# Windowed attention with its backward pass: x loads moved behind the token transpose, gradient loads held by GpSimd

## The chip, the cores and the metric

One core of one Trainium2 chip. The metric is the device time of one execution in microseconds.

## The reference

Windowed self-attention on an image of 256 x 256 tokens with 384 channels, windows of 8 x 8 tokens, one head, all in bfloat16, and its gradients:

```python
xw  = windows of x                       # 1024 windows, 64 tokens, C = 384
q, k, v = split(xw @ wqkv)
p   = softmax(q k^T * C**-0.5)
out = (p @ v) @ wo
# results: out, and the gradients of x, wqkv and wo for a given grad_out
```

## The kernel before

The kernel handles a "quad" of 8 windows (4 tiles of 128 tokens) at a time, 128 quads in all. Weights are multiplied together beforehand (A, B), so a quad needs x and grad_out in two layouts: tokens on the partitions (`xq`, `dq`) and channels on the partitions (`xT`, `dT`). The second layout comes from DMA transposes. The code below is cut and simplified, with my comments. Three quads are under way at once: in one step, quad a (= i+1) is projected, quad b (= i) has its softmax, quad c (= i-1) has its products with the probabilities and its stores.

```python
def load(st):
    st["xq"] = xq = grp.tile([P, QUAD, C], BF16, tag="xq", name="xq", bufs=2 * GQ + 4)
    st["dq"] = dq = qp.tile([P, QUAD, C], BF16, tag="dq", name="dq", bufs=6)
    for t in range(QUAD):
        nc.sync.dma_start(out=xq[:, t, :], in_=windows(x, st, 2 * t))              # SyncE's queue
        nc.gpsimd.dma_start(out=dq[:, t, :], in_=windows(grad_out, st, 2 * t))     # GpSimd's queue

def load_turn(st):      # two DMA transposes on SyncE's queue: dT<-dq, xT<-xq
def to_tokens(st):      # one DMA transpose on SyncE's queue: tok<-yz, 786 KB
def turn(st):           # one DMA transpose on SyncE's queue: PS<-ps, 131 KB

def step(c, b, a, ahead):
    # ... scores, softmax and uv of b; first projection of a (reads dT) ...
    B(turn)
    if ahead is not None:
        load(ahead)                 # quad i+3
    filler(1)
    C_(attend, (0, 1))              # six stores on GpSimd's queue
    # ... second projection of a (reads xT, ends yz) ...
    A(to_tokens)
    filler(1)
    C_(attend, (2, 3))              # six more stores on GpSimd's queue

for i in range(-1, n + 1):
    load_turn(sts[i + 2])           # first in the step
    step(get(i - 1), get(i), get(i + 1), get(i + 3))
    # ... collection of quads for the weight gradients left out ...
```

So SyncE's queue holds, in each step and in this order: dT, xT, PS, four x loads, tok. GpSimd's holds: four gradient loads, six stores, six stores. Both feed the same 16 DMA engines.

Of the kernel before, what the change touches and what calls it, by code (L numbers as in the profile page):

```python
# [11 lines left out]
BF16 = mybir.dt.bfloat16  # L12
F32 = mybir.dt.float32

P = 128
WIN = 8
WT = WIN * WIN
QUAD = 4
# [4 lines left out]
def kernel(  # L23
# [21 lines left out]
    nc = tc.nc  # L45
    _, H, W, C = x.shape
    CK = C // P
    J = 3 * C
# [4 lines left out]
    grp = ctx.enter_context(tc.tile_pool(name="grp", bufs=2 * GQ + 1))  # L53
# [53 lines left out]
    def windows(ap, st, first, count=2):  # L107
        row, col = st["at"]
        return ap[0, row + WIN * first:row + WIN * (first + count), col:col + WIN, :]
# [1 line left out]
    LO, HI = slice(0, WT), slice(WT, P)  # L111
    OTHER = {0: HI, WT: LO}

    def load(st):
        st["xq"] = xq = grp.tile([P, QUAD, C], BF16, tag="xq", name="xq", bufs=2 * GQ + 4)
        st["dq"] = dq = qp.tile([P, QUAD, C], BF16, tag="dq", name="dq", bufs=6)
        for t in range(QUAD):
            nc.sync.dma_start(out=xq[:, t, :], in_=windows(x, st, 2 * t))
            nc.gpsimd.dma_start(out=dq[:, t, :], in_=windows(grad_out, st, 2 * t))  # L119

    def load_turn(st):
        xq, dq = st["xq"], st["dq"]
        st["xT"] = xT = qp.tile([P, QUAD, CK, P], BF16, tag="xT", name="xT", bufs=3)
        st["dT"] = dT = qp.tile([P, QUAD, CK, P], BF16, tag="dT", name="dT")
        for src, dst in ((dq, dT), (xq, xT)):
            k = G_ON_PE if src is dq else 0
            if k < QUAD:
                nc.sync.dma_start_transpose(out=dst[:, k:].rearrange("p t m k -> p (t m) k"),
                                            in_=src[:, k:].rearrange("p t c -> p (t c)"))
# [34 lines left out]

    def to_tokens(st):
        st["tok"] = tok = qp.tile([P, CK, QUAD, 2, P], BF16, tag="tok", name="tok", bufs=3)
        nc.sync.dma_start_transpose(out=tok[:].rearrange("p m t b k -> p (m t b) k"),
                                    in_=st["yz"][:].rearrange("p m t s k -> p (m t s k)"))

    def scores(st):  # L170
        yz, xT = st["yz"], st["xT"]
# [7 lines left out]
    def over_k(ap, n=P):  # L179
        return ap.unsqueeze(2).broadcast_to([n, QUAD, WT])  # L180

    def soft(st, step):
        sd = st["sd"]
        if step == 0:
# [111 lines left out]
    def gf_group(sts):  # L296
        n = len(sts) * QUAD
        for f in range(2):
            for ma in range(CK):
                pw = ring.tile([P, C], F32, tag="r", name="pg")  # L300
                for i in range(n):
                    st, t = sts[i // QUAD], i % QUAD
                    product(pw[:], st["xq"][:, t, ma * P:(ma + 1) * P], st["UW"[f] + "q"][:, t, :], i == 0, i == n - 1)
                nc.vector.tensor_tensor(out=GF_acc[:, f, ma, :], in0=pw[:], in1=GF_acc[:, f, ma, :], op=ALU.add)  # L304
                yield

    def filler(n):
        while n and fill:
            try:
                next(fill[0])  # L310
                n -= 1
            except StopIteration:
                fill.pop(0)

    def step(c, b, a, ahead):


        def on(st):
            return (lambda f, *r: f(st, *r)) if st is not None else (lambda f, *r: None)
        C_, B, A = on(c), on(b), on(a)  # L320
        B(scores)
        B(soft, 0)
        B(uv, 0, 0)
        B(uv, 0, 1)
        B(soft, 1)
        B(uv, 1, 0)
        B(uv, 1, 1)
        B(soft, 2)
        B(soft, 3)
        B(uv, 2, 0)  # L330
        B(uv, 2, 1)
        for t in range(QUAD):
            A(grad_turn, t)
        B(uv, 3, 0)
        B(uv, 3, 1)
        B(soft, 4)
        for mo in range(CK):
            A(project, 0, mo)
        B(soft, 5)
        B(turn)  # L340
        if ahead is not None:
            load(ahead)
        filler(1)
        C_(attend, (0, 1))
        split[0] = True
        for mo in range(CK):
            A(project, 1, mo)
        A(to_tokens)
        filler(1)
        split[0] = ALL  # L350
        C_(attend, (2, 3))
# [3 lines left out]
    quads = [(row, col) for row in range(0, H, 2 * WIN * QUAD) for col in range(0, W, WIN)]  # L355
    sts = [{"at": q, "i": i} for i, q in enumerate(quads)]
    n = len(sts)
    AHEAD = 3
    with tc.manual_schedule(engines=MANUAL):
        for i in range(min(AHEAD, n)):  # L360
            load(sts[i])
            if i < AHEAD - 1:
                load_turn(sts[i])
        held = []
        get = lambda i: sts[i] if 0 <= i < n else None
        for i in range(-1, n + 1):
            if AHEAD - 1 <= i + AHEAD - 1 < n:
                load_turn(sts[i + AHEAD - 1])
            step(get(i - 1), get(i), get(i + 1), get(i + AHEAD) if i >= 0 else None)
            if i > 0:  # L370
                held.append(sts[i - 1])
                sts[i - 1] = None
            if held and (len(held) == GQ or i == n):
                fill.append(gf_group(held))
                held = []
        split[0] = False
        filler(1 << 30)
# [10 lines left out]
            nc.vector.tensor_copy(out=GFT[f][:, mb, :], in_=pt[:])  # L388
    dw_view = out_2.rearrange("(m p) j -> p m j", p=P)
    for ma in range(CK):  # L390
        dw_sb = grp.tile([P, J], BF16, tag="xq", name="dw_sb", bufs=2 * GQ + 4)
        for i, (lhs, rhs, r0) in enumerate(((GFT[0], w_sb, C), (GFb[0], w_sb, 0), (GFT[1], woT_sb, 0))):
            pe = ring.tile([P, C], F32, tag="r")
            for mb in range(CK):
                nc.tensor.matmul(pe[:], lhsT=lhs[:, mb, ma * P:(ma + 1) * P], rhs=rhs[:, mb, r0:r0 + C],
                                 start=(mb == 0), stop=(mb == CK - 1))
            if i < 2:
                nc.scalar.activation(out=dw_sb[:, i * C:(i + 1) * C], in_=pe[:], func=ACT.Copy, scale=scale)
            else:
                nc.vector.tensor_copy(out=dw_sb[:, i * C:(i + 1) * C], in_=pe[:])  # L400
        nc.sync.dma_start(out=dw_view[:, ma, :], in_=dw_sb[:])
# [38 lines left out]
```

## Time and profile before

| | before |
|---|---|
| time, median of the first runs | 1992.8 us (1986.3 to 1994.8) |
| span of the profiled run | 1989.7 us |
| undisturbed step (one quad) | 15.13 us |
| PE busy in such a step | 15.13 us |

The page gives shares over the whole span; the chain and the queue of SyncE give the step. PE is TensorE's matmuls, PEld its weight loads, DVE VectorE, ACT ScalarE, POOL GpSimd and SP SyncE. A row "SPq" of the timeline is an issue by SyncE: its duration is the time for which the issue holds SyncE, and not the time of the transfer (an x load holds it for some 0.6 us and lands 4.1 us after its issue began, in the median). "PE pu <- DMA PS<-ps" in a table of waits means that the matmul that writes pu stood idle until that transfer landed.

### The profile page before, as it was taken

Reading aid. Unit: us, or ns where it says so; the run is one execution under the profiler, and the core shown is the slowest. Engines: PE = TensorE matmul, PEld = TensorE weight load, DVE = VectorE, ACT = ScalarE, POOL = GpSimd, SP = SyncE. Lnnn points to the kernel's source line nnn. Section 1 sums busy time; section 2 is a strip of 40 time slices with the busy share of each in tenths; the row PEclk is TensorE's granted clock in tenths of the full one; section 3 lists DMA queues with packets and bytes.
Section 4 is the critical chain, followed back from the end, with each engine's and each line's share of the span. In section 5 each row is a group of like instructions: output and inputs, shape, how many; then the busy total and the mean of one; then the engine's idle time right before and its main releaser. Section 6 shows DMA issues by size and latency. Waiting matters only on the chain.

```text
span 1989.7 us, 52374 instructions
## 1 busy us (share of the span) xinstructions
PE 1961.3 (99%) x19418; PEld 1122.4 (56%) x19418; DVE 1258.1 (63%) x2851; ACT 1453.4 (73%) x3341; POOL 1122.6 (56%) x2054
## 2 busy tenths in 40 slices
PE   7899999999999999999999999999999999999998
PEld 4455555555555555555555555555555555555555
DVE  4666666666666666666666666566666666666665
ACT  5777777777777777777777777677777777777774
POOL 3555555565556555555655555555555556555543
PEclk9999999999999999999999999999999999999999
DMA  9999999999999999999999999999999999999993
GB/s 202 224 207 222 209 213 226 220 215 225 211 216 223 215 213 214 227 220 217 220 213 219 221 217 210 219 218 223 220 216 216 211 224 214 225 214 219 213 206 102
DMA packets 1042272, 425.62 MB, mean 214 GB/s; under 512 B 925792, under 2 KB 1016672, under 8 KB 1042016
## 3 DMA queue, kind: packets, MB, share of 16 engines
q1 hardware_dynamic: 943312, 270.60, 81.5%
q0 software_dynamic: 98304, 151.39, 31.3%
q8 instruction: 152, 2.49, 0.5%
q14 instruction: 104, 0.85, 0.1%
q10 hardware_dynamic: 400, 0.29, 0.0%
HBM read 101.84 MB, written 101.84 MB: 102 GB/s over the span
## 4 chain that ended last, share of the span: by engine, by line
PE 91%; DMA 7%; ACT 1%; DVE 1%; issue 0%; POOL 0%; SPq 0%; ACTq 0%; POOLq 0%
PE pj L147 33%; PE pj L145 12%; PE pg L147 12%; PE pg L145 12%; PE pd L258 6%; PE pu L253 5%; PE sd L147 5%; PE pw L253 4%; DMA dT<-dq 4%; DMA PS<-ps 2%; ACT uq L229 1%; ACT vq L229 0%; DMA dq<-in_grad_out_dram 0%; DMA xT<-xq 0%; PE pd L253 0%
## 5 line engine op out<-in xcount | busy, mean ns | idle before, releaser
L292 POOL DMA_DIRECT2D out_dram<-o x256 | 139.1, 543 | 693.8 <-ACT o L264 686.4
L304 DVE TENSOR_TENSOR GF_acc<-pg,GF_acc 128x384 f32<-128x384 f32 x258 | 143.8, 557 | 522.5 <-PE pg L145 372.3
L264 ACT CAST o<-po 128x384 bf16<-128x384 f32 x512 | 221.4, 487 | 248.1 <-issue 247.7
L147 PEld LDWEIGHTS <-xT 128*128 128x128 bf16 x3072 | 291.8, 98 | 182.2
L147 PE MATMUL pj<-B_sb,xT 128*128 128x384 bf16 x1536 | 333.4, 326 | 0.0
L147 PE MATMUL pj<-AT_sb,xT 128*128 128x384 bf16 x1536 | 333.3, 326 | 0.0
L119 POOL DMA_DIRECT2D dq<-in_grad_out_dram x512 | 274.2, 548 | 72.5 <-DMA out_dram<-o 39.1
L147 PE MATMUL pj<-dT,BT_sb 128*128 128x512 bf16 x1152 | 269.7, 379 | 5.5 <-DMA dT<-dq 5.3
L145 PE MATMUL pj<-xT,A_sb 128*64 128x512 bf16 x2304 | 271.9, 381 | 1.9 <-DMA xT<-xq 1.8
L229 ACT CAST uq<-pj 128x384 bf16<-128x384 f32 x512 | 247.3, 483 | 31.5 <-PE pj L147 28.4
L229 ACT CAST vq<-pj 128x384 bf16<-128x384 f32 x512 | 250.0, 488 | 2.7 <-ACT uq L229 0.3
L264 ACT CAST d<-pd 128x384 bf16<-128x384 f32 x512 | 227.6, 512 | 0.2 <-ACT o L264 0.2
L147 PEld LDWEIGHTS <-xq 128*128 128x128 bf16 x1572 | 153.7, 98 | 114.8 <-issue 0.3
L145 PEld LDWEIGHTS <-xq 128*64 128x64 bf16 x3000 | 167.9, 110 | 88.9
L207 ACT COPY ps<-Pb 64x256 bf16<-64x256 bf16 x256 | 103.2, 403 | 149.7 <-DVE Pb L204 148.2
L163 ACT CAST yz<-pj 128x512 bf16<-128x512 f32 x384 | 208.5, 659 | 3.6 <-PE pj L145 3.5
L161 ACT CAST yz<-pj 128x512 bf16<-128x512 f32 x384 | 206.4, 645 | 0.3 <-PE pj L147 0.2
L145 PEld LDWEIGHTS <-A_sb 128*64 128x64 bf16 x2304 | 132.4, 110 | 100.2 <-DMA xT<-xq 2.3
L147 PEld LDWEIGHTS <-BT_sb 128*128 128x128 bf16 x1152 | 111.4, 98 | 131.4 <-DMA dT<-dq 11.3
L147 PE MATMUL pg<-Uq,xq 128*128 128x384 bf16 x1032 | 181.6, 326 | 0.0
L253 PE MATMUL pu<-xq,PS 64*64 64x384 bf16 x1024 | 174.9, 335 | 6.4 <-DMA PS<-ps 5.9
L258 PE MATMUL pd<-tok,ps 128*64 128x384 bf16 x1024 | 177.7, 344 | 0.0
(68 smaller groups left out, 3366.6 us busy)
## 6 DMA issues: line engine op xcount, KB each, us to landing
xq<-in_x_dram SPq DMA_DIRECT2D x512, 96.0 KB, 4.1
dq<-in_grad_out_dram POOLq DMA_DIRECT2D x512, 96.0 KB, 4.0
out_dram<-o POOLq DMA_DIRECT2D x256, 96.0 KB, 4.3
out_dram<-o POOLq DMA_DIRECT2D x512, 48.0 KB, 4.4
out_dram<-d POOLq DMA_DIRECT2D x256, 96.0 KB, 4.4
out_dram<-d POOLq DMA_DIRECT2D x512, 48.0 KB, 4.4
dT<-dq SPq DMA_TRANSPOSE x128, 6.6
xT<-xq SPq DMA_TRANSPOSE x128, 6.8
```

The costliest lines, as they stand in the source:

```text
L119: nc.gpsimd.dma_start(out=dq[:, t, :], in_=windows(grad_out, st, 2 * t))
L145: nc.tensor.matmul(out[h], lhsT=lhsT[:, h], rhs=rhs, start=start, stop=stop)
L147: nc.tensor.matmul(out, lhsT=lhsT, rhs=rhs, start=start, stop=stop)
L161: ENG[EV["z"][mo]](out=yz[:, mo, :, 0:4:3, :], in_=pj[:])
L163: ENG[EV["y"][mo]](out=yz[:, mo, :, 1:3, :], in_=pj[:])
L207: nc.scalar.copy(out=ps[h, :, w, :], in_=Pb[h, :, :])
L229: cp(out=dst[:, t, :], in_=pj[:])
L253: nc.tensor.matmul(at[o, :], lhsT=turned(st, lhs, t, h), rhs=st[rhs][h, t, :], **{"start": True, "stop": True, **fl})
L258: nc.tensor.matmul(pd[outer if w == 0 else 1 - outer][o, :], lhsT=st["ps"][:, t, w, :], rhs=st["tok"][:, :, t, w, :], **flags)
L264: nc.scalar.copy(out=sb[:], in_=src[outer][:])
L292: nc.gpsimd.dma_start(out=windows(dst, st, 2 * t0 + 1), in_=sb[:])
L304: nc.vector.tensor_tensor(out=GF_acc[:, f, ma, :], in0=pw[:], in1=GF_acc[:, f, ma, :], op=ALU.add)
```

## The change

The intent is to keep loads away from the large token transpose: the x loads stand behind it in SyncE's queue, and GpSimd is held, by a copy of one element that reads the transpose's first part, until two thirds of it have landed.

```diff
-    def load(st):
-        st["xq"] = xq = grp.tile(..., bufs=2 * GQ + 4)
+    def load(st, behind=None):
+        st["xq"] = xq = grp.tile(..., bufs=2 * GQ + 5)
         st["dq"] = dq = qp.tile(..., bufs=6)
+        if behind is not None:
+            nc.gpsimd.tensor_copy(out=dq[0:1, 0, 0:1], in_=behind[0:1, 0, 0, 0, 0:1])
     ...
     def to_tokens(st):
         st["tok"] = tok = qp.tile([P, CK, QUAD, 2, P], ...)
-        nc.sync.dma_start_transpose(out=tok[:]..., in_=st["yz"][:]...)
+        for m in (slice(0, CK - 1), slice(CK - 1, CK)):
+            nc.sync.dma_start_transpose(out=tok[:, m]..., in_=st["yz"][:, m]...)
     ...
         B(turn)
-        if ahead is not None:
-            load(ahead)
         filler(1)
         C_(attend, (0, 1))
     ...
         A(to_tokens)
+        if ahead is not None:
+            load(ahead, a["tok"])
         filler(1)
     ...
-            step(get(i - 1), get(i), get(i + 1), get(i + AHEAD) if i >= 0 else None)    # AHEAD = 3
+            step(get(i - 1), get(i), get(i + 1), get(i + 4))
```

(The dots and the comment on AHEAD are mine. The loads ahead of the loop are rewritten to the same effect; cut.)

More of the change, by code (lines that the diff above doesn't have):

```diff
@@ L112 @@
     OTHER = {0: HI, WT: LO}
-    def load(st):
-        st["xq"] = xq = grp.tile([P, QUAD, C], BF16, tag="xq", name="xq", bufs=2 * GQ + 4)
+    def load(st, behind=None):
+        st["xq"] = xq = grp.tile([P, QUAD, C], BF16, tag="xq", name="xq", bufs=2 * GQ + 5)
         st["dq"] = dq = qp.tile([P, QUAD, C], BF16, tag="dq", name="dq", bufs=6)
+        if behind is not None:
+            nc.gpsimd.tensor_copy(out=dq[0:1, 0, 0:1], in_=behind[0:1, 0, 0, 0, 0:1])
         for t in range(QUAD):
@@ L166, in to_tokens @@
         st["tok"] = tok = qp.tile([P, CK, QUAD, 2, P], BF16, tag="tok", name="tok", bufs=3)
-        nc.sync.dma_start_transpose(out=tok[:].rearrange("p m t b k -> p (m t b) k"),
-                                    in_=st["yz"][:].rearrange("p m t s k -> p (m t s k)"))
+        for m in (slice(0, CK - 1), slice(CK - 1, CK)):
+            nc.sync.dma_start_transpose(out=tok[:, m].rearrange("p m t b k -> p (m t b) k"),
+                                        in_=st["yz"][:, m].rearrange("p m t s k -> p (m t s k)"))
     def scores(st):
@@ L357 @@
     n = len(sts)
-    AHEAD = 3
     with tc.manual_schedule(engines=MANUAL):
-        for i in range(min(AHEAD, n)):
-            load(sts[i])
-            if i < AHEAD - 1:
-                load_turn(sts[i])
+        load(sts[0])
+        load_turn(sts[0])
+        load(sts[1])
+        load_turn(sts[1])
+        load(sts[2])
         held = []
@@ L366 @@
         for i in range(-1, n + 1):
-            if AHEAD - 1 <= i + AHEAD - 1 < n:
-                load_turn(sts[i + AHEAD - 1])
-            step(get(i - 1), get(i), get(i + 1), get(i + AHEAD) if i >= 0 else None)
+            if 0 <= i < n - 2:
+                load_turn(sts[i + 2])
+            step(get(i - 1), get(i), get(i + 1), get(i + 4))
             if i > 0:
@@ L390 @@
     for ma in range(CK):
-        dw_sb = grp.tile([P, J], BF16, tag="xq", name="dw_sb", bufs=2 * GQ + 4)
+        dw_sb = grp.tile([P, J], BF16, tag="xq", name="dw_sb", bufs=2 * GQ + 5)
         for i, (lhs, rhs, r0) in enumerate(((GFT[0], w_sb, C), (GFb[0], w_sb, 0), (GFT[1], woT_sb, 0))):
```

## The prediction

> **What bounds the kernel now.** I read the page first, then the chain in order of time, two windows of one step each, the waits of PE and the issue queue of SyncE.
>
> The busy row and two of the slice rows of the page:
>
> ```profile
> PE 1961.3 (99%) x19418; PEld 1122.4 (56%) x19418; DVE 1258.1 (63%) x2851; ACT 1453.4 (73%) x3341; POOL 1122.6 (56%) x2054
> ...
> PEclk9999999999999999999999999999999999999999
> DMA  9999999999999999999999999999999999999993
> ```
>
> Two things are full at once: PE (99% of the span, at full clock) and the 16 DMA engines. The chain, in order of time, gives the step:
>
> ```profile
> 168.36 5.84 PE pj L147 x33
> 183.49 5.84 PE pj L147 x33
> 198.62 5.89 PE pj L147 x33
> ```
>
> The same 33 matmuls return every 15.13 us: one quad of windows. The two windows below are one such step each (columns: stretch, length, busy time of PE, PEld, DVE, ACT, POOL, clock, DMA share, GB/s):
>
> ```profile
> 1019.66:1034.79 15.13, 15.13 (x153) 8.70 (x152) 9.70 (x23) 11.29 (x27) 8.78 (x16) 1.00 1.10 218
> 1034.79:1049.92 15.13, 15.13 (x153) 8.69 (x152) 9.70 (x23) 11.29 (x27) 8.79 (x16) 1.00 1.18 193
> ```
>
> PE has no idle time in an undisturbed step, so 15.13 us is a floor that no ordering of transfers can lower. 128 quads x 15.13 = 1936.6 us; the rest of the 1989.7 us span is start, end and disturbed steps. I took the start of the first score matmul of every quad from the trace: from quad 3 on, 20 of 124 steps are longer than 15.15 us, together by 11.9 us. That sum is all that a better order of transfers can win in the steady part: 0.6% of the time. The waits name who made it:
>
> ```profile
> PEld L147 <- DMA dT<-dq: 11.3, 17, 1.5
> PEld L253 <- DMA PS<-ps: 9.0, 12, 3.5
> PE pu L253 <- DMA PS<-ps: 5.9, 5, 3.2
> PE pj L147 <- DMA dT<-dq: 5.3, 9, 1.1
> ```
>
> The gradient transpose (dT) and the probability transpose (PS) come late now and then. (Weight-load and matmul rows show the same late transfer twice and are not to be added.) Why they are late is in SyncE's issue queue:
>
> ```profile
> 1055.64 5.33 SPq L167 DMA_TRANSPOSE tok<-yz  x1
> 1061.19 2.63 SPq L128 DMA_TRANSPOSE dT<-dq  x1
> 1064.00 3.79 SPq L128 DMA_TRANSPOSE xT<-xq  x1
> 1067.95 1.19 SPq L233 DMA_TRANSPOSE PS<-ps  x1
> 1069.20 2.51 SPq L118 DMA_DIRECT2D xq<-in_x_dram  x4
> 1071.82 4.83 SPq L167 DMA_TRANSPOSE tok<-yz  x1
> ```
>
> There is no gap: SyncE issues all the time, about 10.5 us behind the point where the program could have it. The token transpose of a quad is issued at 20.3 us after the start of the step that made its input at 12.8 us. So the queue is not waiting for data; it drains as fast as the DMA engines take it. Over the trace the mean issue times in one step are dT 2.22, xT 3.02, PS 1.50, x 2.73 and tok 4.86 us, 14.3 us, and with about 0.8 us between them the step is full. dT lands at about 17.5 us after its step began and must be there at 19.7 (4.6 us into the next): some 2 us to spare, and the stalls are the steps where that is used up.
>
> **What the Trainium skill says.** "DMA: Bandwidth & Descriptors", section "Queues, rings and completion order", says that each DMA engine round-robins between its queue rows packet by packet. So loads from GpSimd's queue take turns with the transposes of SyncE's. The trace agrees: the token transpose takes between 5.8 and 12.3 us to land (median 8.4) for always the same 786 KB, depending on what runs beside it. "Perfetto Trace Analysis", section "What 'DMA-bound' means", counts as DMA-bound a kernel whose issuing sequencer is a solid row of DMA slices; SyncE's row is that here, beside a full PE. "GPSIMD Engine Reference", section "3.1 Elementwise — side-by-side cycle accounting", gives about 156 ns of dispatch per instruction; no GpSimd copy of one element stands in the trace of before.
>
> **The change part by part.**
> 1. The four x loads (0.6 us of issue each) move from before the token transpose to behind it and are for quad i+4 instead of i+3. Same number and bytes. The token transpose goes 2.7 us earlier in SyncE's cycle, the next dT comes at the same place of the cycle. Cost 0. The buffer count goes from 10 to 11 with the distance, so the buffer waited for is released by the same group of weight-gradient products as before. No new wait.
> 2. The token transpose becomes two. One more issue on a full SyncE. The smallest PS issue, 131 KB, takes 1.19 us, the smallest dT issue, 393 KB, 1.42 us: about 1.1 us is fixed (1.19 less half of the 0.23 that 262 KB more cost). If none were hidden the step would be 16.2 us and the kernel 128 x 1.1 = 140 us slower. But a transpose lands 4 to 5 us after its issue ends, so work is queued in the engines while the next issue is prepared, and the 1.1 us falls into time that SyncE otherwise spends pushed back (tok takes 4.07 us at least, the others 1.2 to 1.5). I take 0.1 us as exposed.
> 3. GpSimd copies one element from the first part of tok into dq: an estimate of 0.2 us from the page's dispatch, on an engine that is busy 8.8 of 15.13 us. Cost 0 on the path.
> 4. The wait. The first part, issued at about 17.6 us of its step, should land near 24.5, 9.4 us into the next step. Then GpSimd issues four gradient loads (4 x 0.55 = 2.2 us), then six delayed stores (3.3 us) and the six of the next half (3.3 us): 9 us of work before the next gate 15.13 us later, so it keeps up. The loads, issued 3.7 us into a step now, go out some 6 us later in relation to the products, but are for one quad further. They land within 7 us, near 31 to 34 us after their step began; their dT is issued at 10.5 us two steps later, at 40.8. Spare 7 us. The stores (2,3) go out 11 us late; their eight buffers last two steps, 30 us. Spare over 10 us.
> 5. The gain. Sorting 120 steps by how far behind SyncE is, its next cycle takes on average 15.52 us where dT is issued before 10.3 us, 15.39 at 10.3 to 10.7, and 15.02 to 15.06 at 11.2 to 12.4. Early, the token transpose runs into the gradient loads; later, it misses them. The gate makes it miss them always. So I expect a natural SyncE cycle near 14.9 us (an estimate: 15.04 less something for the overlap that is still in there, plus the 0.1), below the 15.13 of PE. Then the queue catches up, dT lands well ahead, and the 11.9 us of stalls mostly go.
>
> Sum: 1992.8 less about 9 of the 11.9 us = 1984 us.
>
> **The rivals.**
> *A: the queue gets slower than PE.* The margin of the cycle is about 0.1 to 0.2 us. If the second issue costs more than 0.3 us, or if the now bunched traffic of GpSimd (loads, late stores, next stores in one run of 9 us from the landing of the first part on) slows dT and xT by more than tok gains, the cycle is over 15.13 and every step waits for dT. 15.3 us would be 2005 us or more (0.17 x 128 = 22 us on top of 1984), 15.5 us about 2030. For it: dT follows the x loads directly and so falls into the bunch. Against it: bytes and their kinds are unchanged, and the engines never were empty.
> *B: nothing moves.* The late steps come in bursts (steps 14 to 18, 79 to 82, 100 to 103, 120 to 124), each beginning with a step in which everything lands 2 to 5 us late at once. If something outside the order of these transfers causes them, they stay, and the time is 1990 to 1994.
> *C: the gate starves the gradient.* dq arrives too late for dT and the wait for dT becomes one for dq. It needs the 7 us of spare to go; then each step would lose, and I would see over 2050. Unlikely.
> *D: over 2% faster.* That is below 1953 us, and without any stall the kernel needs 1992.8 - 11.9 = 1981, perhaps 1978 if the first steps fill better. It would need PE to be shorter, and no matmul is changed.
>
> **Range and chances.** The low end is the floor with a little for the spread of runs (before: 1986.3 to 1994.8): 1977. The high end allows rival A with a cycle of about 15.3 us: 2010. Faster by over 2%: 0.01. Slower by over 2% (over 2032.7, a cycle of 15.5): 0.05. Within: 0.94.
>
> **What would show each step.** PE still 15.13 us in an undisturbed step; if that moved, the reading of the bound is wrong. Right on the gain: PE waits for dT and PS below 5 us, SyncE showing gaps or real waits before tok or PS, dT issued earlier than 10.5 us, tok landing (first issue to last landing) below 8 us. Step 2 wrong: the two tok issues together above 5.5 us while SyncE stays solid. Step 4 wrong: dT or PE waiting for the gradient load, or ACT waiting for an output buffer. Rival A: over half of the steps longer than 15.2 us with dT as releaser. What would make the prediction wrong altogether is a DMA cycle that leaves 15.13 us upward, since PE has nothing left to give.

## The result, and the profile after

The changed kernel takes 2101.5 us (2091.3 to 2104.4, 4 runs) against 1993.8 us of the kernel before in the same rounds: ratio 1.0537, with a 95% interval of 1.0494 to 1.0579. It is slower by 5.4%. (A ratio here is the mean time of one kernel's fast runs over the mean of the other's fast runs of the same rounds, so it is not quite the ratio of the medians quoted beside it.)

The busy row of the page after, and the waits of PE:

```profile
PE 1979.7 (95%) x19418; PEld 1117.3 (53%) x19418; DVE 1258.0 (60%) x2851; ACT 1457.3 (70%) x3341; POOL 1140.0 (55%) x2179
```

```profile
PE pu L256 <- DMA PS<-ps: 40.5, 40, 2.0
PE pj L149 <- DMA dT<-dq: 39.7, 47, 3.0
```

PE has the same 19418 matmuls and is now idle for 5% of the span. It waits for the same two transposes as before (5.9 and 5.3 us then). From quad 3 on, 92 of 124 steps are longer than 15.2 us (17 before), and all that exceeds 15.13 us adds up to 110 us (11.9 before). The other steps still take 15.13 us. So the floor has not moved; the queue in front of it has become slower than it. SyncE's queue, one cycle of the kernel after, from token transpose to token transpose:

```profile
1060.42 5.32 SPq L170 DMA_TRANSPOSE tok<-yz  x2
1065.79 2.57 SPq L120 DMA_DIRECT2D xq<-in_x_dram  x4
1068.60 1.45 SPq L130 DMA_TRANSPOSE dT<-dq  x1
1070.10 3.13 SPq L130 DMA_TRANSPOSE xT<-xq  x1
1073.39 2.28 SPq L236 DMA_TRANSPOSE PS<-ps  x1
1075.76 5.12 SPq L170 DMA_TRANSPOSE tok<-yz  x2
```

The row is still solid. In the mean over the steps of quads 20 to 110, from the start of one issue to the next:

| us per step | dT | xT | PS | tok | x loads | cycle |
|---|---|---|---|---|---|---|
| before | 2.33 | 3.20 | 1.54 | 5.15 | 2.97 | 15.18 |
| after | 1.96 | 3.68 | 1.92 | 5.34 | 3.15 | 16.05 |

The landing times say the same (transposes of the table of issues, before and then after; last column: median us from issue to landing):

```profile
xT<-xq SPq DMA_TRANSPOSE x128, 6.8
tok<-yz SPq DMA_TRANSPOSE x128, 8.4
PS<-ps SPq DMA_TRANSPOSE x128, 5.0
```

```profile
tok<-yz SPq DMA_TRANSPOSE x256, 5.4
...
xT<-xq SPq DMA_TRANSPOSE x128, 8.2
PS<-ps SPq DMA_TRANSPOSE x128, 5.6
```

(5.4 is for each of tok's parts; from the first part's issue to the last landing it is 7.9 us.) The token transpose gained half a microsecond, xT lost 1.4 and PS 0.6. PS has a deadline too: it landed 21.3 us after the start of its step before and 25.2 after (medians of the trace), and an undisturbed step reads it at 24.0.

And GpSimd's queue after, at the gate that waits for the token transpose issued at 1060.42 above:

```profile
1067.32 0.18 POOL L118 COPY dq<-tok 1x1 bf16<-1x1 bf16 x1 [2.24 <-PE pj L147]
1067.89 2.14 POOL L121 DMA_DIRECT2D dq<-in_grad_out_dram  x4 [0.39 <-POOL dq L118]
1069.98 0.57 POOL L295 DMA_DIRECT2D out_dram<-o  x1
```

The four x issues run from 1065.79 to 1068.36. GpSimd issues its loads only from 1067.89 on, then the held stores: their data move when SyncE is at dT, xT and PS. What does that leave beside the x loads? Four windows of 3 us before and four after, each beginning about 1 us after the first issue of a row of x loads (last two columns: mean busy share of the 16 DMA engines, GB/s):

```profile
977.47:980.47 3.00, 3.00 (x18) 1.59 (x17) 2.23 (x6) 1.78 (x6) 2.92 (x6) 1.00 0.98 234
992.50:995.50 3.00, 3.00 (x18) 1.57 (x16) 2.13 (x6) 1.78 (x5) 2.73 (x6) 1.00 0.97 268
1007.98:1010.98 3.00, 3.00 (x18) 1.57 (x16) 2.45 (x7) 1.81 (x5) 2.37 (x5) 1.00 0.89 229
1022.98:1025.98 3.00, 3.00 (x17) 1.56 (x16) 2.32 (x7) 1.78 (x6) 2.52 (x5) 1.00 1.10 204
```

```profile
1018.52:1021.52 3.00, 3.00 (x44) 1.83 (x41) 0.43 (x1) 1.39 (x3) 1.74 (x4) 1.00 1.16 148
1034.86:1037.86 3.00, 3.00 (x36) 1.80 (x32) 0.04 (x1) 1.87 (x5) 0.33 (x2) 1.00 1.15 140
1051.24:1054.24 3.00, 3.00 (x43) 1.68 (x40) 1.21 (x3) 1.01 (x4) 1.67 (x4) 1.00 0.87 159
1066.79:1069.79 3.00, 3.00 (x36) 1.79 (x32) 0.04 (x1) 1.87 (x5) 2.08 (x5) 1.00 0.88 189
```

204 to 268 GB/s before, 140 to 189 after. (The share counts a packet where it starts and is noisy over 3 us; the bytes are plain.) POOL is busy issuing for 2.4 to 2.9 of the 3 us before and 0.3 to 2.1 after: most of the missing bytes are GpSimd's. I laid the packets of 90 such rows over one another and took how busy the engines were in each microsecond, counted from the first x issue; in brackets, the part of GpSimd's queue. Over 1.00 means that packets overlap in an engine, and a stretch of transposes alone reaches 1.25.

| microsecond after the first x issue | 1 to 2 | 2 to 3 | 3 to 4 | 4 to 5 |
|---|---|---|---|---|
| before | 1.12 (0.57) | 1.04 (0.59) | 0.99 (0.52) | 0.99 (0.43) |
| after | 1.05 (0.04) | 0.82 (0.05) | 0.74 (0.18) | 0.86 (0.39) |

In the changed kernel the DMA engines run partly dry behind every row of x loads.

### The profile page after: what moved, and what is told of

Its sections match the earlier page's. It is cut to its first block, busy times and chain, and to the rows that moved or that the text cites. A ratio compares the mean times of both kernels' runs of the same rounds, so it can differ in the third digit from the quotient of the medians.

```text
span 2089.5 us, 52866 instructions
## 1 busy us (share of the span) xinstructions
PE 1979.7 (95%) x19418; PEld 1117.3 (53%) x19418; DVE 1258.0 (60%) x2851; ACT 1457.3 (70%) x3341; POOL 1140.0 (55%) x2179
## 5 line engine op out<-in xcount | busy, mean ns | idle before, releaser
L149 PE MATMUL pj<-dT,BT_sb 128*128 128x512 bf16 x1152 | 270.3, 380 | 54.2 <-DMA dT<-dq 39.7
L118 POOL COPY dq<-tok 1x1 bf16<-1x1 bf16 x125 | 22.1, 177 | 538.4 <-PE pj L147 302.2
L147 PE MATMUL pj<-xT,A_sb 128*64 128x512 bf16 x2304 | 278.0, 387 | 0.1
L256 PE MATMUL pu<-xq,PS 64*64 64x384 bf16 x1024 | 174.7, 335 | 41.1 <-DMA PS<-ps 40.5
L149 PEld LDWEIGHTS <-BT_sb 128*128 128x128 bf16 x1152 | 106.3, 98 | 195.1 <-DMA dT<-dq 82.5
L292 POOL DMA_DIRECT2D out_dram<-o x256 | 148.6, 581 | 90.0 <-DMA dq<-in_grad_out_dram 31.9
L295 POOL DMA_DIRECT2D out_dram<-o x256 | 141.3, 552 | 92.8 <-DMA dq<-in_grad_out_dram 52.7
```

The source lines that it names most:

```text
L147: nc.tensor.matmul(out[h], lhsT=lhsT[:, h], rhs=rhs, start=start, stop=stop)
L149: nc.tensor.matmul(out, lhsT=lhsT, rhs=rhs, start=start, stop=stop)
L256: nc.tensor.matmul(at[o, :], lhsT=turned(st, lhs, t, h), rhs=st[rhs][h, t, :], **{"start": True, "stop": True, **fl})
L292: nc.gpsimd.dma_start(out=windows(dst, st, 2 * t1 + 1, 1), in_=sb[LO, :])
L295: nc.gpsimd.dma_start(out=windows(dst, st, 2 * t0 + 1), in_=sb[:])
```

## The experiments

All 16 kernels are correct. The first theories were: **issue** (the second issue of the token transpose costs time on a full SyncE), **gate** (holding GpSimd bunches its traffic), **order** (the new place of the loads costs). Four kernels take the parts away one by one. (The diffs are cut to the lines that matter; the splitting of `load` into `load_x` and `load_d` is left out.)

**split_only**: the kernel before, with only the split.

```diff
-        nc.sync.dma_start_transpose(out=tok[:]..., in_=st["yz"][:]...)
+        for m in (slice(0, CK - 1), slice(CK - 1, CK)):
+            nc.sync.dma_start_transpose(out=tok[:, m]..., in_=st["yz"][:, m]...)
```

> The kernel before with the token transpose in two issues (2/3 and 1/3) and nothing else changed. Theory 'issue': the second issue costs the full SyncE queue some 0.8 us a step, so 2070 to 2100 us, and the two issues of tok together take over 5.6 us. Theories 'gate' and 'order': the extra issue hides in the backpressure, 1985 to 2000 us.

Measured: 2029.1 us (before 1995.1), ratio 1.0151, 95% interval 1.0102 to 1.0200. Between the two: the split costs something, less than the issue theory asked. The two issues of tok do not take longer than the one did (5.00 us against 5.15, from start to next start). The dT behind them takes 0.63 us longer (2.96 against 2.33) and PS 0.29, while xT takes 0.42 less: 0.3 us a step in all. PE then waits for PS above all (30.5 us in the trace, against 7.2 for dT).

**no_gate**: the changed kernel without the copy.

```diff
-            load(ahead, a["tok"])
+            load(ahead)
```

> The changed kernel without GpSimd's copy: the gradient loads stand at their new place in GpSimd's program (behind the first half's stores) but wait for no transpose; the split and the new place of the x loads stay. Theory 'gate': the loss is gone, 1985 to 2000 us. Theories 'issue' and 'order': still 2080 to 2105 us.

Measured: 2094.0 us, ratio 1.0495 (1.0452 to 1.0537). The gate is not the cause of the loss. Taking it away wins nothing that this run can tell from noise.

**whole_gate**: the changed kernel with one token transpose, all of which GpSimd waits for.

```diff
-        for m in (slice(0, CK - 1), slice(CK - 1, CK)):
-            nc.sync.dma_start_transpose(out=tok[:, m]..., in_=st["yz"][:, m]...)
+        nc.sync.dma_start_transpose(out=tok[:]..., in_=st["yz"][:]...)
```

> The changed kernel with the token transpose in one issue again; GpSimd then waits for all of it. Theory 'issue': 1985 to 2010 us. Theory 'gate': as slow or slower than the changed kernel, 2095 to 2130 us, since the gate opens about 1.5 us later. Theory 'order': 2085 to 2105 us.

Measured: 2031.0 us, ratio 1.0172 (1.0134 to 1.0209). All three theories missed: a gate that opens later is much better, though not good.

**order_only**: both of these edits; only the place of the loads is new.

> No split and no gate: only the loads moved behind the token transpose, four quads ahead. Theories 'issue' and 'gate': 1980 to 2000 us. Theory 'order' (x loads directly ahead of dT and xT, gradient loads behind the stores): 2085 to 2105 us.

Measured: 2074.9 us, ratio 1.0395 (1.0354 to 1.0436). PE waits 52.5 us for PS and 23.3 for dT. Most of the loss, 80 of 106 us, is in the part that I had called free: the order. With 2075 as the base, the whole gate wins 44 us and the split costs 19; both together lose 27.

So the order had to be taken apart. The second round's theory was **slot**: four x issues take 2.7 us whatever runs beside them, so GpSimd's traffic is free there and costs time beside transposes.

**x_only**: only the x loads go behind the token transpose; the gradient loads keep their place.

```diff
         B(turn)
-        if ahead is not None: load(ahead)            # x and gradient, i+3
+        if near is not None: load_d(near)            # gradient, i+3
     ...
         A(to_tokens)
+        if ahead is not None: load_x(ahead)          # x, i+4
```

> No split, no gate: only the x loads go behind the token transpose, four quads ahead; the gradient loads keep their old place in GpSimd's program, three ahead. Theory 'slot' (the issue of the x loads takes 2.7 us whatever runs beside it, so GpSimd's traffic that falls there is free, and what falls beside the transposes lengthens them): the gradient loads at 4 to 6 us of the step now fall beside tok and not beside x, so 2030 to 2080 us, with under 1.0 us of GpSimd's queue beside the x issues (1.6 before). Theory 'late loads' (what costs is that the gradient loads are issued at the end of the step, behind the stores): 1985 to 2005 us.

Measured: 2026.0 us, ratio 1.0149 (1.0123 to 1.0175), just below the slot theory's range; 0.94 us of GpSimd's queue beside the x issues, as it expected. Here the engines do not run dry behind the row: laid over one another as above, they are 1.19, 1.10, 1.04 and 1.03 busy in its second to fifth microsecond. This half of the order costs some 28 us in another way (see the sums below).

**dq_only**: the other half, x loads at the old place, gradient loads behind the first half's stores.

```diff
         B(turn)
-        if ahead is not None: load(ahead)
+        if near is not None: load_x(near)            # x, i+3
     ...
         A(to_tokens)
+        if ahead is not None: load_d(ahead)          # gradient, i+4
```

> No split, no gate: only the gradient loads go to their new place in GpSimd's program, four quads ahead; the x loads stay ahead of the token transpose, three ahead. Theory 'slot': the gradient loads leave the x loads and fall beside dT and xT at the end of the step, so 2030 to 2080 us and under 1.0 us of GpSimd's queue beside the x issues. Theory 'x order' (what costs is that the x loads stand directly ahead of dT): 1985 to 2005 us.

Measured: 1987.0 us, ratio 0.9949 (0.9919 to 0.9979): not slower but slightly faster. The expectation failed in its arithmetic, not in its rule: when the gradient loads go later, the stores behind them do too, and 1.70 us of GpSimd's queue still lies beside the x issues (1.61 in the kernel before). Neither half of the order costs 80 us. Together they do, because only together do they leave the row of x loads alone: in order_only 0.47 us of GpSimd's queue lies beside it.

**gate_PS**: the new order, no split, and the gate opens earlier, when PS has landed.

```diff
-            load(ahead, a["tok"])        # GpSimd waits for the token transpose of quad a
+            load_x(ahead)
+            load_d(ahead, b["PS"][0:1, 0, 0, 0:1])       # GpSimd waits for PS of quad b
```

> The changed order in one token transpose, with GpSimd's copy waiting for the probability transpose of the step instead of the token transpose: the gate opens some 3 to 4 us earlier, when the x loads are about to be issued, so that gradient loads and x loads move side by side. Theory 'slot': GpSimd's queue beside the x issues rises above 1.2 us, and the time goes below the kernel with the gate on the whole transpose (2031 us): 1990 to 2025 us. Theory 'bunch' (any holding of GpSimd costs): 2031 us or more.

Measured: 2004.8 us, ratio 1.0039 (1.0005 to 1.0074); 1.11 us of GpSimd's queue beside the x issues. In the slot theory's range of time, a little under its share. Holding GpSimd costs little (0.4%) if it is let go when the x loads start. Among the kernels with a row and no split, GpSimd's share beside the row and the time go together roughly: 0.47 us and 2075 (order_only), 0.94 and 2026 (x_only), 1.1 and 2031 (whole_gate), 1.11 and 2005, 1.61 and 1995 (before), 1.70 and 1987 (dq_only). In whole_gate that share must be stores, for its gradient loads may start only after tok has landed, 9.6 us after its issue, and by then the row has been issued.

**split_three**: the kernel before with the token transpose in three issues.

```diff
-        for m in (slice(0, CK - 1), slice(CK - 1, CK)):      # as in split_only
+        for m in (slice(0, 1), slice(1, 2), slice(2, 3)):
```

> The kernel before with the token transpose in three issues. If an extra transpose issue has a cost of its own (34 us for the first one, measured), a second extra issue doubles it: 2055 to 2075 us. If the 34 us came from the change of phase alone, the third issue adds little: 2020 to 2040 us.

Measured: 2035.6 us, ratio 1.0195 (1.0169 to 1.0221). That is 38 us over its kernel before, against 34 for two issues: the third adds nothing clear of noise. The split's cost is not a price per issue.

The third round tests the cause behind the slot. The theory **underfed**: an x issue takes 0.6 us for 98 KB, so SyncE supplies 393 KB in 2.7 us, 146 GB/s, while the kernel as a whole moves 217 GB/s; in a row of four the work queued in the engines runs out.

**x_eight**: the kernel before with the x loads in eight issues of 49 KB.

```diff
-            nc.sync.dma_start(out=xq[:, t, :], in_=windows(x, st, 2 * t))
+            for h, half in enumerate((LO, HI)):
+                nc.sync.dma_start(out=xq[half, t, :], in_=windows(x, st, 2 * t + h, 1))
```

> The kernel before with the x loads in eight issues of one window each, 49 KB, in place of four. Theory 'underfed': the row of x issues grows from 2.7 to some 5 us and feeds the engines at half the rate, GpSimd's traffic covers only a part: 2060 to 2200 us. Theory 'mixing': the same bytes at the same place, 1990 to 2020 us.

Measured: 2362.2 us, ratio 1.1837 (1.1793 to 1.1880), above the range that the theory gave. A cycle of its queue:

```profile
1003.94 5.13 SPq L119 DMA_DIRECT2D xq<-in_x_dram  x8
1009.17 5.55 SPq L168 DMA_TRANSPOSE tok<-yz  x1
```

Half the bytes take the same 0.6 us of SyncE: eight issues take 5.13 us where four took 2.5. The engines are still 1.14 and 1.08 busy in the second and third microsecond of the row and fall to 0.73, 0.47 and 0.33 in the fourth to sixth. The row is 2.5 us longer than before, the step 3.1. The same bytes, in the same place of the queue, cost 18% because they are issued in smaller pieces. The rival "mixing", that asked for 1990 to 2020 us, is out as the only cause.

**spread**: the kernel before with one x load behind each of the four transposes. (A sketch of the queue, not the code; the same in after_spread.)

```diff
-   SyncE's queue:  dT  xT  PS  x0 x1 x2 x3  tok
+   SyncE's queue:  dT  x0  xT  x1  PS  x2  tok  x3
```

> The kernel before with its four x loads spread over SyncE's queue, one behind each of the four transposes, instead of four in a row; the gradient loads stay. Theory 'underfed' (four x issues in a row, 0.6 us each for 98 KB, feed the 16 DMA engines too slowly; only traffic of GpSimd at that moment keeps them full): each single issue is covered by the transpose ahead of it, SyncE's cycle falls below 15.0 us, the stalls of PE go: 1977 to 1990 us. Theory 'mixing' (loads beside transposes slow these, so x loads and gradient loads must meet): 2010 us or more.

Measured: 2038.3 us, ratio 1.0207 (1.0178 to 1.0237), five rounds. The theory underfed missed this one wholly. The engines are well fed here, and yet SyncE's cycle is 15.5 us. What grew is the work: see the table of sums below.

**after_spread**: the same spread in the changed kernel, split and gate left as they are.

```diff
-   SyncE's queue:  dT  xT  PS  tok(2/3)  tok(1/3)  x0 x1 x2 x3
+   SyncE's queue:  dT  x1  xT  x2  PS  x3  tok(2/3)  tok(1/3)  x0
```

> The changed kernel (split, gate on the first two thirds, four ahead) with its x loads spread, one behind each transpose. Theory 'underfed': the low stretch of the DMA engines behind the x issues (0.74 to 0.86 busy) is gone, and with it most of the loss: 1985 to 2040 us, where the upper end is the cost of the split alone. Theory 'bunch' (held and late traffic of GpSimd beside dT and xT is the cost): 2080 us or more.

Measured: 1979.1 us (1978.5 to 1981.3), ratio 0.9915 (0.9892 to 0.9938), five rounds: faster than both kernels, below the expected range. Its queue, one cycle:

```profile
1010.93 5.90 SPq L174 DMA_TRANSPOSE tok<-yz  x2
1016.88 0.93 SPq L118 DMA_DIRECT2D xq<-in_x_dram  x1
1018.04 2.48 SPq L132 DMA_TRANSPOSE dT<-dq  x1
1020.57 0.58 SPq L118 DMA_DIRECT2D xq<-in_x_dram  x1
1021.25 1.55 SPq L132 DMA_TRANSPOSE xT<-xq  x1
1022.85 0.98 SPq L118 DMA_DIRECT2D xq<-in_x_dram  x1
1023.93 1.29 SPq L240 DMA_TRANSPOSE PS<-ps  x1
```

dT and xT together are issued in 4.0 us, 4.6 in the cycle shown of the kernel after. The queue catches up: dT is issued 10.2 us after the start of the step in step 6, 3.2 us in step 16, and stays near there (medians: 3.6 here, 11.1 in the kernel before, where the prediction says about 10.5, and 14.1 in the one after). That is 0.70 us gained per step, a cycle of some 14.4 us as long as nothing holds it. Then the token transpose waits for its own input (its issue begins at 12.3 us of the step, as the second third of yz is written; it was 21.5 in the changed kernel), and PE, over its steps, only for itself: 2 of 124 steps are longer than 15.15 us.

That left open which part of the change the spread made useful. Three more kernels complete the table.

**spread_no_gate**: after_spread without GpSimd's copy.

```diff
-            load_d(ahead, a["tok"])
+            load_d(ahead)
```

> The changed kernel with its x loads spread, and GpSimd's copy left out (the split stays). Theory 'both' (a row of x issues starves the DMA engines, and gradient loads beside the token transpose lengthen it; the gate cures only the second and shows its worth once the first is cured): slower than the spread kernel with the gate (1979 us) by 10 to 60 us. Theory 'feed alone': the same within 6 us.

Measured: 2070.3 us, ratio 1.0366 (1.0304 to 1.0427). Slower, as the theory 'both' said, but by 91 us and not by 10 to 60.

**spread_whole_gate**: after_spread with the token transpose in one issue (the edit of whole_gate).

> The changed kernel with its x loads spread and the token transpose in one issue, so that GpSimd waits for all of it. If the split has a cost of its own wherever it stands (34 us in the kernel before), SyncE's slack must hide it in the spread kernel and nothing is to be seen: 1977 to 1984 us, with the token transpose issued no later. If the opening after two thirds is what makes the gate work, 1990 us or more.

Measured: 1977.0 us (1976.7 to 1977.9), ratio 0.9904 (0.9857 to 0.9951). The fastest by its median, though it and after_spread were not timed in the same rounds. Within the first range; opening after two thirds is not what makes the gate work.

**spread_order**: both edits.

> The changed kernel with its x loads spread, no split, no gate: the loads' places alone. Theory 'both': 1990 to 2040 us. Theory 'feed alone': 1977 to 1985 us.

Measured: 2037.5 us, ratio 1.0213 (1.0144 to 1.0282), at the upper end of the range of 'both'. It loads four quads ahead and spread three, and both take the same time (2037 and 2038 us), so the distance is not likely to matter; no run changed it alone.

**split_reverse**: a last look at the split: the kernel before, one third of the token transpose first, two thirds last.

```diff
-        for m in (slice(0, CK - 1), slice(CK - 1, CK)):      # as in split_only
+        for m in (slice(0, 1), slice(1, CK)):
```

> The kernel before with the token transpose in two issues, one third first and two thirds last. With two thirds first the gradient transpose behind it took 0.6 us longer to issue, in two parts as in three (where the last part is one third as well). If a short last part is what costs, this one is near the kernel before: 1990 to 2010 us. If any cut of the token transpose costs: 2022 to 2040 us.

Measured: 1997.2 us (before 1998.5), ratio 0.9998 (0.9975 to 1.0022). And **split_dT**, run with the third round, with the gradient transpose in two issues:

```diff
-            nc.sync.dma_start_transpose(out=dst[:]..., in_=src[:]...)
+            for g in (slice(0, 2), slice(2, 4)) if src is dq else (slice(0, 4),):
+                nc.sync.dma_start_transpose(out=dst[:, g]..., in_=src[:, g]...)
```

> The kernel before with the gradient transpose, not the token transpose, in two issues. If any additional transpose issue costs what the split of tok cost, 2025 to 2040 us; if that cost belongs to tok's place and phase, 1990 to 2010 us.

Measured: 1996.2 us, ratio 1.0000 (0.9968 to 1.0031). So one more transpose issue costs nothing by itself in these two places. A short piece at the end of the token transpose, directly ahead of dT, costs 34 us.

### The table that they make

Medians in us, loads at their new place in all eight; the kernel before was at 1994 to 1998 in these rounds:

| | x loads in a row | x loads spread |
|---|---|---|
| no split, no gate | 2075 | 2037 |
| split, no gate | 2094 | 2070 |
| no split, gate on all of tok | 2031 | 1977 |
| split, gate on the first two thirds | 2101 (the change) | 1979 |

The gate is worth 44 us with the row and no split, 60 with the spread and no split, 91 with spread and split, and nothing in the one combination that the change chose.

Two sums from the traces sort the kernels. A packet is one piece of a transfer in the trace (256 bytes in a transpose). Add up the time of all DMA packets of a step and divide by 16 engines: that is the work. Divide the work by the step: that is how full the engines are. This is bookkeeping: it tells which of the two moved, not why. Packets overlap in an engine, so a packet's time can hold waiting for others; and where PE sets the step (15.13 us), fullness says only how much work there was.

| | step, us | packet time, us | fullness |
|---|---|---|---|
| before | 15.18 | 17.55 | 1.156 |
| after | 16.03 | 17.79 | 1.110 |
| no_gate | 16.06 | 17.78 | 1.107 |
| split_only | 15.49 | 17.90 | 1.155 |
| x_only | 15.50 | 18.36 | 1.184 |
| dq_only | 15.22 | 17.93 | 1.178 |
| order_only | 15.85 | 17.62 | 1.112 |
| whole_gate | 15.52 | 17.37 | 1.119 |
| gate_PS | 15.23 | 16.93 | 1.112 |
| x_eight | 18.24 | 18.39 | 1.008 |
| spread | 15.53 | 18.29 | 1.177 |
| spread_order | 15.55 | 18.09 | 1.163 |
| spread_no_gate | 15.75 | 18.19 | 1.155 |
| spread_whole_gate | 15.13 | 17.32 | 1.145 |
| after_spread | 15.13 | 17.33 | 1.145 |

A row of x loads with nothing beside it goes with a low fullness (after, no_gate, order_only), and so does a row of eight issues (x_eight). That is not the whole cause: x_only and split_only are as full as the kernel before or fuller and lose some 30 us because the work grew, and gate_PS is as little full as order_only and loses almost nothing because its work is the least of all. Spreading the x loads restores the fullness, but without a gate the work goes up: a 256-byte packet of a transpose takes 27.3 ns on average in spread and 25.5 in spread_whole_gate, and with 6656 such packets on 16 engines in a step, 1.8 ns are 0.75 us.

A gate takes work back in three of the four pairs (17.62 to 17.37, 18.09 to 17.32, 18.19 to 17.33; 17.78 to 17.79 in the fourth), and not by a faster token transpose. From order_only to whole_gate (each time first without, then with the gate):

```profile
dT<-dq SPq DMA_TRANSPOSE x128, 6.6
...
tok<-yz SPq DMA_TRANSPOSE x128, 7.6
```

```profile
dT<-dq SPq DMA_TRANSPOSE x128, 5.2
...
tok<-yz SPq DMA_TRANSPOSE x128, 9.6
```

| median us to landing, without and with the gate | dT | xT | tok |
|---|---|---|---|
| row, no split | 6.6, 5.2 | 8.2, 7.8 | 7.6, 9.6 |
| row, split | 6.7, 6.6 | 8.4, 8.2 | 7.4, 7.9 |
| spread, no split | 5.3, 4.9 | 7.6, 5.3 | 8.9, 9.4 |
| spread, split | 5.4, 4.2 | 8.0, 6.1 | 8.3, 8.4 |

With the gate tok lands no earlier in any pair; dT and xT land earlier, clearly so wherever the gate pays. Less of GpSimd's packet time then lies beside dT and beside xT in all four pairs (in the first, 2.8 us over 16 engines beside dT without the gate and 1.3 with it), and more beside tok in three (2.0 and 3.4). Why that is the better place no run here shows. Spread or gate alone does not suffice; the two kernels that have both, spread and gate, are the two that beat the kernel before clearly.

## Why the prediction was wrong

- **Bound: right.** Undisturbed steps still take 15.13 us, and the two best kernels, at 1977 and 1979 us, stand at or a little below the 1981 us that I had given for a kernel without stalls.
- **Part 1, "Cost 0": this is the step that failed.** I counted issues and bytes and found none added. Moving the x loads alone costs 28 us (x_only), moving the gradient loads alone gains some 10 (dq_only), and moving both costs 80 (order_only). The row of x loads is a stretch in which SyncE alone does not keep the engines full (0.74 busy at the least); in the kernel before, gradient loads and stores happened to fill it (1.61 us of GpSimd's queue beside it), after the change they do not (0.46). That this is all of the 80 us is not shown: the 28 us of x_only come with full engines and longer packets. The path was incomplete as well: I counted the spare of dT (some 2 us) and never that of PS, which was 2.7 us (landed at 21.3, read at 24.0), and PE waits for PS at least as long as for dT (40.5 and 39.7 us after; 52.5 and 23.3 in order_only).
- **Part 2, "0.1 us as exposed": mis-sized.** The split costs 34 us by itself in the kernel before, 0.27 us a step, and 19 and 33 us in the two pairs of the table without a gate. My reasoning, that a second issue hides in the backpressure, holds for split_reverse and split_dT, which cost nothing; it is the short last part that does not hide. I also looked for the cost in tok's own issues, whose bound of 5.5 us was not reached (5.2): it lies in dT and PS. (The smallest tok issue of the trace is 3.90 us, not 4.07.)
- **Parts 3 and 4: right in their waits.** The copy takes 0.18 us, PE never waits for a gradient load, and no wait of ACT for a store's buffer shows. That 0.2 us was forecast is luck: it rested on a page's figure for another engine. Part 4 asked only whether the gradient loads come in time, not what they had been filling.
- **Part 5, the gain: a gate can pay, but not for the reason given.** I took from the trace that a token transpose which misses the gradient loads makes a faster cycle. The sorting does not carry that: the groups left out take 15.14 us (dT issued at 10.7 to 11.2) and 15.21 (later than 12.4), so the cycle does not go on falling; and as SyncE's lag stays bounded, an early step must on average be followed by a longer cycle, whatever the cause. Nor was a gate needed for it: the new place alone takes the gradient loads off tok (the flights of the four loads overlap tok's by 14.1 us together in the kernel before, 2.9 in order_only, 4.3 in whole_gate). The 44 to 91 us that a gate wins elsewhere come with tok landing no earlier and dT and xT earlier.
- **Rival A's outcome was what happened, and I gave it 5%.** Its reason, the held traffic of GpSimd, was not needed: without the gate the loss is the same (no_gate). Its sentence that the bunched traffic "slows dT and xT by more than tok gains" describes xT (6.8 to 8.2 us) and PS (5.0 to 5.6); dT did not slow. Against it I had put that "the engines never were empty". That held for the order before and was taken for a property of the kernel. The range ended at 2010 us because I thought of cycles up to 15.3 us only; it was 16.0.
- **Rival B: did not come.** The time moved, and the late steps vanish once SyncE has slack (after_spread). What starts a burst is not shown.

What stays open: why a short transpose ahead of dT lengthens dT's issue by 0.6 us (the packet time of a step rises from 17.55 to 17.90 us at the same fullness); why the packet time differs between orders of the same transfers at all; and why the gate at two thirds is worth nothing with a row of x loads. That it opens 1.5 us after the first x issue in the cycle shown, too late for the row and early enough for dT, fits, but no run moved that moment alone: gate_PS moved it and had no split.

## What to carry to other kernels

When an engine's issue queue is a solid row, look at how many bytes each issue puts into the DMA engines per microsecond, not only at how long it takes: here short issues in a row let the engines run partly dry unless another queue's traffic lay beside them. A long transfer ahead of each of them kept the engines full, but helped the time only together with a gate (1977 and 1979 us, against 2037 and 2070 without). Moving such a row is not free even though no transfer is added, because it changes what lies beside it. Where a change consists of several parts, try them in all combinations: here the gate was worth nothing in the combination chosen and was the best part of another, and one further edit (one x load behind each transpose) turned a loss of 5.4% into a gain of about 0.9%.

## What the Trainium skill lacked or had wrong

- "DMA: Bandwidth & Descriptors", section "Issuing engines are not separate DMA queues", says that issuing from several engines only saves sequencer time, which is "usually small relative to the DMA itself". Here it is not small: an x issue takes 0.6 us for 98 KB, against 0.45 us for these bytes at 217 GB/s (an estimate from the profile: 3.3 MB in a step of 15.18 us), and with 49 KB pieces the same 0.6 us made the kernel 18% slower.
- The same page has nothing on what a transfer's neighbours in the same queue do to it. Four x loads in a row and four x loads with a transpose ahead of each differ by 122 us (2101 and 1979) in the changed kernel, and by some 40 us the other way in the kernel before (1997 and 2038), with the same transfers.
- No page has that a short last piece of a split transpose costs more than a short first piece: 2029 us against 1997.
- "Perfetto Trace Analysis", section "What 'DMA-bound' means", treats full engines and a solid sequencer as separate bounds. In the changed kernel SyncE's row is solid and the engines fall to 0.74 busy within each step: the two bounds take turns.
